# GraphSAGE aggregation: each broadcast of source indices for 28 buckets is split into two transfers of 14 buckets

## The chip, the core and the metric

The kernel runs on one core of a Trainium2 chip. The metric is the device time of one execution in microseconds (us). The core has a matrix engine (PE; its weight loads are listed apart as PEld), a vector engine (DVE), a scalar engine (ACT), GpSimd (POOL) and a sync engine (SP) that in this kernel does little but start DMA transfers. Sixteen DMA engines move all data between the memory (HBM) and the core's on-chip buffers; they also bring the instructions that the engines execute.

## What is computed

```python
def reference(x, src, dst, deg_inv, w_self, w_neigh):
    N = x.shape[0]
    nsum = _segment_sum(x[src], dst, N)
    h_neigh = nsum * deg_inv[:, None]
    return x @ w_self + h_neigh @ w_neigh
```

There are 12,500 nodes with 64 features and 800,000 edges. For each node the features of its in-neighbours are summed (gather by `src`, add by `dst`), scaled, multiplied by a 64x64 matrix, and added to the node's own features times another 64x64 matrix.

## The kernel before

The kernel sorts the edges into buckets and then does the gather and the sum with matrix products.

**Sort.** Each edge becomes a 32-bit key that holds its bucket: a block of 160 destination nodes and a block of 128 source nodes. 128 rows of keys are sorted on DVE and ACT (`sort_runs`), cut up, gathered again by indirect DMAs on POOL (`gather_runs`, L391), merged (`merge_runs`, L413 and L453), and cut into windows, one per bucket (`find_and_gather`, L603). This is done in two parts; part 0 is ready at about 815 us of the profiled execution, and part 1 is merged while the node sums already run.

**Lists in memory.** `decode_buckets` writes for each bucket 128 source positions as bf16 numbers to the tensor `sl` in memory (L652), 256 bytes per bucket, and keeps the destination positions on chip in `dlT`.

**Sums over nodes.** `nodes` walks over the 7,644 buckets in tiles of 8. For each tile PE does 8 products (L850) of a one-hot matrix of source positions (`ohs`) with a block of features (`xh`), which gathers the rows of 128 edges per bucket into the PSUM tile `ct`; ACT (L860) or, from tile 503 on, in turn DVE (L858) copies `ct` to `xg`; and PE does 16 products (L905) with the one-hot matrix of destination positions (`ohd`), which add the rows into the sums `acc`. Edges that did not fit a bucket come in as rows `lx`, gathered by POOL (L869) and added by L885. The finished sums go through `finish` (L968 to L976), which also loads `fo` on SP (L952) and stores `out`.

**One-hots, the place of the change.** `one_hots` makes both one-hot matrices for 28 buckets at a time, 273 times. SP starts a transfer (L819) that reads the 28 x 256 = 7,168 bytes of `sl` once for each of the 128 partitions, so that each partition of `slb` holds all 3,584 source positions; that is 128 rows of 7,168 bytes, or 896 KB. DVE then compares `slb` with the partition's number (L821, `ohs`) and `iota` with `dlT` (L824, `ohd`). `slb` has three buffers, so SP may run two groups ahead, and the transfer for a buffer is started when L821 of three groups earlier has ended.

**What sets the order.** From the merge on, the order of instructions on each engine is the order in which the program emits them (`manual_schedule` in `after_sort`). `nodes` yields once per tile, and between two yields `sums_and_merge` puts a portion of the merge of part 1, of its windows, of the decoding, or of the left-over edges. Waits between engines are on semaphores; each transfer that SP starts counts on one of eight semaphores, taken in turn.

Of the kernel before, what the change touches and what calls it, by code (L numbers as in the profile page):

```python
# [258 lines left out]
class Kernel:  # L259
# [552 lines left out]
    def one_hots(self, pool):  # L812


        nc = self.nc
        for c in range(0, NBID, 28):
            b = pool.tile([128, 28 * 128], BF, name="slb", bufs=3)
            src = self.sl[c:c + 28]
            nc.sync.dma_start(b, bass.AP(tensor=src.tensor, offset=src.offset, ap=[[0, 128], [1, 28 * 128]]))  # L819
            s = pool.tile([128, 28, 128], FH, name="ohs", bufs=3)  # L820
            nc.vector.tensor_scalar(s.rearrange("p c s -> p (c s)"), b, self.pidx[:, :1], None, op0=OP.is_equal)  # L821
            d = pool.tile([128, 14, HN, 2], FH, name="ohd", bufs=5)
            ix = self.dlT[:, c:c + 28].rearrange("p (c t) -> p c t", t=2)[:, :, None, :].to_broadcast([128, 14, HN, 2])
            nc.vector.tensor_tensor(d, self.iota[:, None].to_broadcast([128, 14, HN, 2]), ix, op=OP.is_equal)  # L824
            yield [(s[:, j], d[:, j // 2, :, j % 2]) for j in range(28)]
# [377 lines left out]
```

## Time and profile before

| | us |
|---|---|
| median of 3 runs (1891.56 to 1901.67) | 1899.85 |
| the profiled execution | 1899.66 |
| its span in the trace | 1897.9 |
| PE busy (matrix products) | 972.7 |
| DVE busy | 1672.6 |
| ACT busy | 1176.5 |
| POOL busy | 809.3 |
| first and last start of L819 | 821.6 and 1870.4 |

The profile is of one execution, in microseconds from the start of its span. Busy time is the time in which an engine executes; the share of busy time is an average over stages that have different limits. The first 815 us are the sort, in which PE does little; the sums over nodes take the rest. In that rest the DMA engines are mostly busy: the transfers of `slb` are by far the largest.

```profile
DMA  4322000001100012257677877889768887888884
...
slb<-sl SPq DMA_DIRECT2D x273, 896.0 KB
```

The first row gives, for 40 equal slices of the span, the mean busy share of the 16 DMA engines in tenths; the second the number and size of the transfers of L819. A row of waits names the engine that was idle, the line it was about to run, and what it was released by; "issue" there means that the profile shows nothing that it waited for. DMA queues are named by number: q1 holds what SP starts, q0 what POOL starts, q10 what ACT starts, and q8 and q14 instructions for the engines (187 packets of 16 KB and 62 of 8 KB).

### The profile page before, as it was taken

What the parts mean: (1) busy time and instruction counts of PE and PEld (TensorE: products, weight loads), DVE (VectorE), ACT (ScalarE), POOL (GpSimd) and SP (SyncE); (2) the same over time, 40 slices, a digit from 0 to 9 for tenths busy, and PEclk for the clock granted to TensorE, in tenths of its full rate; (3) what the DMA queues carried; (4) which work ended last, traced back from release to release, by engine and by line L of the source; (5) the groups of instructions that cost most, each with busy time, mean ns of one, the idle gap of its engine ahead of it and who ended that gap; (6) DMA issues with size and microseconds to landing.
All of it is one profiled execution on the core that took longest, in us unless ns stands there. A gap on an engine that the chain in (4) does not pass through costs nothing.

```text
span 1897.9 us, 54529 instructions
## 1 busy us (share of the span) xinstructions
PE 972.7 (51%) x23659; PEld 841.7 (44%) x23659; DVE 1672.6 (88%) x1760; ACT 1176.5 (62%) x1853; POOL 809.3 (43%) x917
## 2 busy tenths in 40 slices
PE   0043000000000000039888888898879989998997
PEld 0033000000000000038777777787768877787886
DVE  7999999997749998779699999999799888788885
ACT  7463019205510022549888898898968878777886
POOL 1000000699889984898521331326554123322431
PEclk9995555555555555569999999999989999999999
DMA  4322000001100012257677877889768887888884
GB/s 152 70 68 68 0 32 0 26 20 52 22 20 10 10 40 66 58 190 279 207 240 245 244 256 257 245 267 322 234 206 283 285 255 263 242 266 265 273 259 139
DMA packets 104804, 305.24 MB, mean 161 GB/s; under 512 B 52945, under 2 KB 60491, under 8 KB 103915
## 3 DMA queue, kind: packets, MB, share of 16 engines
q1 hardware_dynamic: 86347, 277.44, 41.2%
q0 software_dynamic: 17632, 22.17, 8.6%
q8 instruction: 187, 3.06, 0.6%
q10 hardware_dynamic: 576, 2.07, 0.3%
q14 instruction: 62, 0.51, 0.1%
HBM read 282.20 MB, written 19.41 MB: 159 GB/s over the span
## 4 chain that ended last, share of the span: by engine, by line
DVE 43%; PE 23%; POOL 16%; issue 11%; DMA 3%; ACT 3%; DVEq 0%; SPq 0%; POOLq 0%; ACTq 0%
DVE u L453 15%; PE ct L850 13%; POOL u L391 12%; PE acc L905 9%; DVE a L227 7%; DVE b L227 7%; DVE ohd L824 6%; DVE ohs L821 4%; POOL pad L304 2%; POOL v L603 1%; ACT xg L860 1%; DMA slb<-sl 1%; PE po L968 1%; DVE u L413 1%; POOL lx L869 1%
## 5 line engine op out<-in xcount | busy, mean ns | idle before, releaser
L860 ACT ACTIVATE xg<-ct 128x1024 f16<-128x1024 f32 (+1 forms) x898 | 853.3, 1032 | 166.8 <-PE ct L850 135.3
L850 PE MATMUL ct<-xh,ohs 128*128 128x128 f16 x7644 | 543.1, 223 | 64.3 <-DVE ohs L821 27.3
L850 PEld LDWEIGHTS <-ohs 128*128 128x128 f16 x7644 | 449.0, 100 | 107.7 <-issue 57.5
L391 POOL DMA_INDIRECT u<-d,ix x256 | 362.2, 1415 | 217.1 <-DVE ix L383 175.4
L905 PE MATMUL acc<-ohd,xg 64*128 64x80 f16 x15288 | 405.5, 199 | 72.8 <-issue 49.1
L453 DVE TENSOR_TENSOR u<-u 128x1456 f32<-128x1456 f32 (+46 forms) x292 | 393.7, 1377 | 21.6 <-issue 14.6
L905 PEld LDWEIGHTS <-xg 64*128 64x128 f16 x15288 | 318.6, 96 | 144.6 <-issue 70.4
L824 DVE TENSOR_TENSOR ohd<-iota,dlT 128x2240 f16<-128x2240 bf16 x273 | 360.2, 1319 | 0.0
L869 POOL DMA_INDIRECT lx<-xt,lsrc x140 | 236.8, 1691 | 263.2 <-PE acc L885 224.4
L821 DVE TENSOR_SCALAR ohs<-slb,pidx 128x3584 f16<-128x3584 bf16 x273 | 315.0, 1154 | 34.4 <-PE ct L850 21.7
L381 PE MATMUL stp<-idf,st 128*128 128x128 f32 x2 | 0.9, 447 | 356.8 <-DVE st L379 356.8
L227 DVE TENSOR_TENSOR a<-b 128x608 f32<-128x608 f32 (+44 forms) x124 | 174.0, 1445 | 4.6
L227 DVE TENSOR_TENSOR b<-a 128x608 f32<-128x608 f32 (+44 forms) x124 | 173.9, 1444 | 4.3
L976 POOL DMA_DIRECT2D out<-o x25 | 23.6, 946 | 354.7 <-DVE o L975 288.4
L381 PEld LDWEIGHTS stp<-idf,st 128*128 128x128 f32 x2 | 0.4, 182 | 357.3 <-issue 357.3
L660 PE MATMUL tr<-idb,l 128*128 128x128 bf16 x60 | 8.2, 278 | 285.2 <-issue 240.9
L858 DVE CAST xg<-ct 128x1024 f16<-128x1024 f32 x64 | 78.3, 1224 | 70.2 <-PE ct L850 69.5
L660 PEld LDWEIGHTS <-l 128*128 128x128 bf16 x60 | 5.0, 119 | 288.2 <-issue 244.3
L418 ACT ACTIVATE u<-u 128x30 f32<-128x30 f32 (+34 forms) x136 | 29.8, 268 | 143.6 <-DVE u L453 74.5
L229 ACT ACTIVATE b<-a 128x1 f32<-128x1 f32 (+21 forms) x52 | 18.7, 383 | 135.3 <-DVE a L227 130.2
L597 ACT ACTIVATE junk<-u,c 128x166 bf16<-128x166 f32 (+36 forms) x37 | 26.7, 722 | 119.1 <-DVE u L453 119.0
L603 POOL DMA_INDIRECT v<-d,ix x60 | 77.8, 1297 | 47.5 <-ACT ix L622 35.0
(153 smaller groups left out, 868.7 us busy)
## 6 DMA issues: line engine op xcount, KB each, us to landing
slb<-sl SPq DMA_DIRECT2D x273, 896.0 KB
u<-d,ix POOLq DMA_INDIRECT x256
xt<-xh SPq DMA_DIRECT2D x1, 3136.0 KB
fo<-own SPq DMA_DIRECT2D x26, 120.0 KB
own<-os SPq DMA_DIRECT2D x12, 256.0 KB
out<-o POOLq DMA_DIRECT2D x24, 120.0 KB
lx<-xt,lsrc POOLq DMA_INDIRECT x140
rd<-dst SPq DMA_DIRECT2D x4, 521.0 KB
```

The source lines that it names most:

```text
L227: nc.vector.tensor_tensor(view(dst, lo + sh, [[st, g], [1, l]]), x, y, op=op)
L304: self.nc.gpsimd.memset(self.pad, 0.0)
L391: nc.gpsimd.indirect_dma_start(out=u[:nr, EDGE + p * w:EDGE + (p + 1) * w], out_offset=None, in_=src, in_offset=bass.IndirectOffsetOnAxis( ...
L453: nc.vector.tensor_tensor(view(dst, EDGE + o + out, d), view(src, EDGE + o + x, d), view(src, EDGE + o + x + gap, d), op=op)
L603: self.nc.gpsimd.indirect_dma_start(out=self.v[:, k].bitcast(F32), out_offset=None, in_=flat(self.d2[home(part, k)], 128 * PITCH2[home(par ...
L821: nc.vector.tensor_scalar(s.rearrange("p c s -> p (c s)"), b, self.pidx[:, :1], None, op0=OP.is_equal)
L824: nc.vector.tensor_tensor(d, self.iota[:, None].to_broadcast([128, 14, HN, 2]), ix, op=OP.is_equal)
L850: nc.tensor.matmul(ct[:, i * 128:(i + 1) * 128], cols[i][0], self.xh[:, (b0 + i) % NB].rearrange("p a f -> p (a f)"), start=True, stop=True)
L858: nc.vector.tensor_copy(xg[:, :cnt * 128], ct[:, :cnt * 128])
L860: nc.scalar.activation(xg[:, :cnt * 128], ct[:, :cnt * 128], AF.Copy)
L869: nc.gpsimd.indirect_dma_start(out=x, out_offset=None, in_=self.xt, in_offset=bass.IndirectOffsetOnAxis(ap=self.left[p][1][:, c:c + 1], ax ...
L905: nc.tensor.matmul(acc[h][:, db % OCT * HN:(db % OCT + 1) * HN], xg[r, i * 128:(i + 1) * 128], d[r], start=db % OCT == 0 and sb == 0, stop ...
```

## The change

Each group's transfer is issued as two: the first brings the positions of the first 14 buckets into the first half of each partition of the `slb` buffer, the second those of the other 14 into the second half. Rows are 3,584 bytes long in place of 7,168, and there are 546 transfers of 128 rows in place of 273. Buffers, their number, and what is computed are unchanged.

```diff
         for c in range(0, NBID, 28):
             b = pool.tile([128, 28 * 128], BF, name="slb", bufs=3)
-            src = self.sl[c:c + 28]
-            nc.sync.dma_start(b, bass.AP(tensor=src.tensor, offset=src.offset, ap=[[0, 128], [1, 28 * 128]]))
+            for j in range(0, 28, 14):
+                src = self.sl[c + j:c + j + 14]
+                nc.sync.dma_start(b[:, j * 128:(j + 14) * 128],
+                                  bass.AP(tensor=src.tensor, offset=src.offset, ap=[[0, 128], [1, 14 * 128]]))
             s = pool.tile([128, 28, 128], FH, name="ohs", bufs=3)
```

All later lines of the kernel stand two lines lower than before. The order of instructions on PE, DVE, ACT and POOL is the same. On SP, at the start of the sums, the order before was (`fo` are the loads of `finish`):

```order
L652 DMA sl<-l_2277 128x128
L819 DMA slb<-sl 128x3584 x25
L952 DMA fo<-own 120x4x64
L819 DMA slb<-sl 128x3584 x4
L952 DMA fo<-own 120x4x64
L819 DMA slb<-sl 128x3584 x17
```

and it is now:

```order
L652 DMA sl<-l_2277 128x128
L820 DMA slb<-sl 128x1792 x50
L954 DMA fo<-own 120x4x64
L820 DMA slb<-sl 128x1792 x8
L954 DMA fo<-own 120x4x64
L820 DMA slb<-sl 128x1792 x34
```

Each transfer of a group has become two in the same place, and nothing has moved past them. On DVE, in the later part of the sums, two groups stood like this, with the semaphores that each instruction waits for in brackets (DMAHW are those of SP's transfers):

```order
L821 TENSOR_SCALAR ohs<-slb,pidx 128x3584 [waits DMAHW4_49]
L824 TENSOR_TENSOR ohd<-iota,dlT 128x2240
L877 TENSOR_SCALAR ohl<-wide,lp_2754 128x320
L821 TENSOR_SCALAR ohs<-slb,pidx 128x3584 [waits DMAHW5_49,PE_49]
L824 TENSOR_TENSOR ohd<-iota,dlT 128x2240
```

and stand now:

```order
L823 TENSOR_SCALAR ohs<-slb,pidx 128x3584 [waits DMAHW4_49,DMAHW3_49]
L826 TENSOR_TENSOR ohd<-iota,dlT 128x2240
L879 TENSOR_SCALAR ohl<-wide,lp_2760 128x320
L823 TENSOR_SCALAR ohs<-slb,pidx 128x3584 [waits DMAHW6_49,DMAHW5_49,PE_49]
L826 TENSOR_TENSOR ohd<-iota,dlT 128x2240
```

The comparison that makes `ohs` waits for one more semaphore, since it needs both halves.

## The prediction

> **What bounds the kernel now.** The change touches only the sums over nodes, from about 820 us on, so I read that part by stretches: busy time of each engine, then the waits, then the chain of work that ended last.
>
> ```profile
> core 0: us, PE busy (x) PEld busy (x) DVE busy (x) ACT busy (x) POOL busy (x), PEclk, DMA share, GB/s
> 1400.00:1500.00 100.00, 91.79 (x2285) 79.70 (x2285) 88.39 (x117) 79.44 (x91) 31.25 (x18) 0.95 0.75 257
> 1500.00:1600.00 100.00, 89.37 (x2340) 78.15 (x2340) 82.84 (x90) 80.08 (x89) 25.06 (x19) 1.00 0.81 265
> 1600.00:1700.00 100.00, 90.44 (x2254) 79.09 (x2252) 82.26 (x90) 76.43 (x84) 31.43 (x22) 0.95 0.83 257
> 1700.00:1800.00 100.00, 89.57 (x2359) 78.39 (x2357) 84.86 (x94) 80.95 (x88) 30.19 (x20) 1.00 0.85 270
> 1800.00:1890.00 90.00, 79.92 (x2070) 69.67 (x2068) 66.87 (x72) 72.38 (x80) 22.30 (x15) 0.98 0.69 212
> 1000.00:1270.00 270.00, 233.57 (x5976) 204.02 (x5974) 269.69 (x246) 234.85 (x268) 68.32 (x34) 0.97 0.80 252
> ```
>
> From 1000 to 1270 us, where the merge of part 1 runs beside the sums, DVE is busy for 269.69 of 270 us: nothing that frees another engine helps there. From 1400 us on no engine is full, PE is nearest (441 of 490 us, the sum of its five rows), and the DMA engines are busy for 0.69 to 0.85 of the time. What PE waits for in that stretch is this (line, releaser: us in total, times, longest):
>
> ```profile
> PE acc L905 <- issue: 25.0, 30, 2.4
> PE ct L850 <- issue: 14.8, 9, 3.2
> PE ct L850 <- ACT xg L860: 1.7, 7, 0.3
> ```
>
> 441 busy and 39.8 us of "issue" make 481 of 490: PE is the bound, and its only large wait is one for which the profile names no releaser. The chain of waits of the same stretch runs over PE too, and its longest pieces are such waits:
>
> ```profile
> 1553.86 2.49 issue
> 1734.33 3.17 issue
> ```
>
> What PE lacks there is its instructions. The page counts them and the packets that bring them:
>
> ```profile
> PE 972.7 (51%) x23659; PEld 841.7 (44%) x23659; DVE 1672.6 (88%) x1760; ACT 1176.5 (62%) x1853; POOL 809.3 (43%) x917
> ...
> q8 instruction: 187, 3.06, 0.6%
> ```
>
> 2 x 23,659 instructions over 187 packets is 253 for each packet of 16 KB; that q8 serves PE I take from PE having nine tenths of all instructions. PE runs some 22,600 instructions (both x columns) from 1400 to 1890 us, 89 packets' worth, and stops 39 times, for 1.02 us on average. So nearly every second packet comes late.
>
> Why late? Here is a stretch of 10 us: two gathers that POOL issues and two of PE's stops, then the packets of each DMA queue in four windows, 1554.3 to 1557, 1557 to 1558, 1559.1 to 1560.8 and 1560.8 to 1562 us (packets, MB, share of the time of 16 engines).
>
> ```profile
> 1552.94 1.33 POOL L869 DMA_INDIRECT lx<-xt,lsrc  x1 [4.22 <-PE acc L885]
> 1559.63 0.95 POOL L869 DMA_INDIRECT lx<-xt,lsrc  x1 [5.36 <-PE acc L885]
> ...
> 1556.34 0.23 PE L850 MATMUL ct<-xh,ohs 128*128 128x128 f16 x1 [2.49 <-issue]
> ...
> 1563.11 0.29 PE L905 MATMUL acc<-ohd,xg 64*128 64x80 f16 x6 [1.85 <-issue]
> ```
>
> ```profile
> q1 hardware_dynamic: 124, 0.86, 94.4%
> ...
> q1 hardware_dynamic: 36, 0.15, 68.9%
> q0 software_dynamic: 31, 0.03, 59.1%
> ...
> q1 hardware_dynamic: 90, 0.54, 75.5%
> ...
> q0 software_dynamic: 22, 0.03, 36.1%
> q1 hardware_dynamic: 5, 0.03, 5.7%
> q8 instruction: 1, 0.02, 4.9%
> ```
>
> The gather issued at 1552.94 us (done on POOL at 1554.27) has no packet at all while the rows of an `slb` transfer move; its packets come when the transfer ends, after 1557. The next one, and the one instruction packet, again come only after 1560.8, when q1 runs dry, and PE's stop at 1563.11 follows. The DMA engines do not alternate row by row: **other queues get their turn when a transfer's rows on an engine, 8 of 128, are through.** A row takes 0.944 x 16 x 2.7 / 124 = 0.33 us, so a turn of `slb` lasts about 2.6 us. Each instruction packet that is asked for during a turn waits for its end.
>
> [...]
>
> **The change part by part.**
>
> *Turns of half the length (gain).* 8 rows of 3,584 bytes take half of 2.6 us, so an instruction packet waits up to 1.3 us less. The 30 stops at L905 average 0.83 us and would mostly go; the 9 at L850 average 1.64 us and would shrink to about a fifth. If every late packet met a whole turn, 30 x 0.75 + 9 x 1.3 = 34 us would go; many meet part of one, or two. I take two thirds of 39.8 us, **-27 us**, between 0 (turns do not shorten) and -39.8. Room for it is there: in 463 us DVE's 405 us (sum of its five rows) are 88% and ACT's 389 us 84%. From 1000 to 1270 us the same cure is worth 0, since DVE is full.
>
> ```profile
> PE acc L905 <- issue: 7.9, 11, 2.2
> ...
> 844.00 2.44 DMA u<-d,ix
> ...
> 1351.88 6.29 DMA tk<-d
> ```
>
> Between 1270 and 1400 us PE has 7.9 us of the same waits (first row), and the chain has a small load of POOL that takes 6.29 us (third row, 7 KB): POOL's queue waits for turns as well. PE is only partly the bound there; I take **-3 us**, between 0 and -11. The gathers before the merge end with 2.44 us of DMA on the chain (second row): **-1 us**, between 0 and -2.4.
>
> *273 more transfers to issue (cost).* Rows for this and the next points: the issue itself, what SP waits for, what DVE waits for at L821, semaphore instructions there, the start of the sums, and a window (115 to 140 us) with rows of 256 bytes only.
>
> ```profile
> L819 SPq DMA_DIRECT2D slb<-sl x273: 319/320/516, 821.6 to 1870.4; - x137
> SPq L819 <- DVE ohs L821: 819.5, 254, 10.0
> DVE ohs L821 <- DMA slb<-sl: 9.9, 4, 5.0
> L821 DVEq EVENT_SEMAPHORE  x214: 21/21/50, 817.9 to 1875.7; - x107
> 826.42 1.15 DVE L821 TENSOR_SCALAR ohs<-slb,pidx 128x3584 f16<-128x3584 bf16 x1 [5.01 <-DMA slb<-sl]
> 829.32 1.22 DVE L821 TENSOR_SCALAR ohs<-slb,pidx 128x3584 f16<-128x3584 bf16 x1 [0.51 <-DMA slb<-sl]
> ...
> q1 hardware_dynamic: 10651, 2.71, 42.2%
> ```
>
> 273 x 0.32 = 87 us on SP, which waits 819.5 us at this line: hidden. Behind it in SP's queue stand only the loads `fo` and the next groups. The second half is issued 0.32 us after the first, whose rows move for 1.3 us, so it is not late: 0. Without that cover each group would land 0.32 us later, 87 us over 273 groups.
>
> *Twice the rows (cost).* The 256-byte rows take 0.422 x 16 x 25 / 10,651 = 0.016 us each, which bounds the fixed part of a row from above; below, it is 0. 273 x 128 more rows are at most 0.13 us per group on each engine, 35 us in all beside a period of (1870.4 - 821.6) / 272 = 3.86 us per group. The DMA share would go from 0.8 to at most 0.84. What hides it is the lead of two groups: 269 of 273 groups were there when DVE wanted them. Exposed is the first group, for which DVE waits 5.01 us, and the next: **+0.5 us**; a late landing here and there, **+1 us**; if the cover were gone, +35.
>
> *One more semaphore at L821 (cost).* At most 273 x 0.05 = 14 us. DVE has 214 such instructions at L821 now and is yet busy 269.69 of 270 us, so they run under the instruction before: 0. Behind L821 stand L824 and the copies L858, for which PE waits; exposed, all 14 would count.
>
> **Sum**, against the profiled execution's own 1899.66 us, which is the median of the runs (1899.85) within 0.2: -27 - 3 - 1 + 0.5 + 1 = -29.5, **1870 us**.
>
> [...]
>
> **The rivals.**
>
> *No change: the turn is not a transfer.* If an engine counts rows or bytes and takes both halves in one turn when both are queued (the second is queued after 0.32 us, so they always are), instruction packets wait as long as before and only +0.5 + 1 is left: **1901 us**. For it: the rows above show transfers of 8 rows per engine and cannot tell a limit of 8 rows from one of 16. Against: in the four windows the other queues come in when a transfer is through, though the next groups follow closely.
>
> *Slower: the second half is held up by the turns it gives away.* Every group now yields once in its middle. A turn of POOL's queue is priced by this stretch (1500 to 1700 us):
>
> ```profile
> q0 software_dynamic: 1347, 1.82, 11.4%
> ```
>
> 0.114 x 16 x 200 / 1,347 = 0.27 us; with 0.13 for the rows, 0.4 us per group. It decides where DVE reaches L821 with less than that in hand. If a third of the groups did, 91 x 0.4 = 36 us is lost at L821, DVE falls behind PE, and half of the gain (13) is left: **1923 us**. Against: only 4 waits for `slb` in the row above, and 2 of them are at the start.
>
> *Much slower: the fixed part of a transfer is paid twice in a row.* The first group takes 826.42 - 821.6 = 4.8 us, the next lands 2.9 us after it; 1.9 us are fixed. Were halves to run one after the other, a group would take 2 x 1.9 + 2.9 = 6.7 us where DVE takes one every 3.86: 273 x 2.9 = 780 us more, **2680 us**. Against: the second group already overlaps the first's fixed part. [...]
>
> **How the numbers follow.** Forecast 0.67, no change 0.19, held up 0.13, paid twice 0.01. The forecast's own range is 1852 (all of 39.8, 6 more before 1400) to 1889. A measurement of this kernel can tell about 0.5%, 9.5 us, from no change. Faster by more is the forecast but for its weak end: 0.66; within: 0.21; slower: 0.13. The range that holds 8 in 10 goes from 1852 over the no-change case: 1852 to 1904.
>
> **What would show it.** Right: PE's "issue" waits from 1400 us on fall from 39.8 to some 13 us, their longest from 3.2 to under 2; PE's busy share there rises over 0.94; gathers' packets appear between the halves; 1000 to 1270 us keeps its length. Wrong: the same "issue" waits (rival one), or `slb` as releaser of L823 tens of times (rival two). The prediction falls if instruction packets are late for another reason than turns, or if DVE or ACT, at 88% and 84%, take over before PE has gained.

## The result and the profile after

The change makes the kernel slower by about 0.8%: a median of 1916.28 us over 10 runs (1906.84 to 1931.02) against 1901.03 us over 10 runs of the kernel before (1891.56 to 1906.39), a ratio of 1.0079 with a 95% interval from 1.0054 to 1.0103. The prediction said 1870 us and a range of 1852 to 1904. The profiled execution of the change took 1915.36 us, 15.7 more than that of before; its span is 1913.6 us.

The busy time of each engine by stretches, as shown for the kernel before:

```profile
core 0: us, PE busy (x) PEld busy (x) DVE busy (x) ACT busy (x) POOL busy (x), PEclk, DMA share, GB/s
1400.00:1500.00 100.00, 83.75 (x2143) 73.24 (x2139) 89.53 (x143) 75.52 (x85) 35.67 (x21) 0.95 0.79 251
1500.00:1600.00 100.00, 87.78 (x2222) 77.33 (x2223) 78.86 (x85) 76.28 (x85) 25.29 (x18) 0.96 0.82 254
1600.00:1700.00 100.00, 87.29 (x2258) 76.47 (x2257) 80.43 (x89) 76.95 (x86) 32.12 (x19) 0.98 0.81 248
1700.00:1800.00 100.00, 87.35 (x2237) 76.70 (x2235) 81.95 (x90) 76.99 (x83) 29.12 (x21) 0.95 0.84 262
1800.00:1890.00 90.00, 82.90 (x2149) 72.95 (x2147) 75.56 (x83) 73.72 (x80) 27.09 (x19) 0.98 0.85 262
1000.00:1270.00 270.00, 231.92 (x5996) 201.70 (x5988) 269.73 (x245) 239.11 (x272) 62.06 (x34) 0.98 0.81 251
```

DVE is as full from 1000 to 1270 us as it was (269.73 of 270). From 1400 us on PE is busy for 429 of 490 us, where it was 441: its share fell from 0.90 to 0.88 and did not rise over 0.94. (These stretches are the same in time, not in work: the change reaches each group of buckets some microseconds later.)

The waits of that same stretch in the change (line, releaser: us in total, times, longest):

```profile
ACT xg L862 <- PE ct L852: 100.4, 121, 4.1
DVE xg L860 <- PE ct L852: 76.0, 45, 4.7
...
PE acc L907 <- issue: 30.8, 22, 3.1
...
PE ct L852 <- issue: 15.9, 13, 2.9
```

PE's waits without a releaser are 46.7 us in place of 39.8. This view lists 35 of them in place of 39, but it counts short waits of other kinds too. The stops can also be counted where a block of 256 PE instructions ends (weight loads and products together). The traces show this length: there is one packet on q8 for every 253 PE instructions (47,318 over 187), and from 1400 to 1890 us 26 of the 43 gaps over 0.4 us in PE's weight loads stand at one and the same place in a count of 128 weight loads in the kernel before, 35 of 43 in the change, and no other place has more than two. In time, 39.0 of the 49.2 us of such gaps in the later part of the sums stand at the ends of blocks in the kernel before, 52.6 of 64.9 in the change. With gaps of 0.15 us or more, the change has 42 such stops in place of 30 in this stretch (worked out from the two traces). The two longest pieces without a releaser on the chain of waits are about as long as before (3.17 and 2.60 there):

```profile
1581.61 3.13 issue
...
1747.79 2.86 issue
```

To see where the 15.7 us lie, the starts of the `ohs` comparison (L821, now L823) can be compared group by group, since the program does the same in both. Worked out from the two traces, in us:

```
groups         before   change
0 to 36         150.8    155.4
36 to 108       278.0    278.0
108 to 144      149.1    151.6
144 to 272      474.9    482.5
```

The stretch in which DVE is full keeps its length to a tenth. In the first row gathers of `lx` land late: on the chain from 822 to 965 us three of them take 5.5 to 6.4 us in the change, and one of 6.1 in the kernel before. A second execution of the change has only one (6.4 us), and its first row is 151.4 us. The loss that stays is in the last two rows (152.2 and 480.2 us in that second execution), above all in the last, in which PE is the bound.

### The profile page after: what moved, and what is told of

Read it like the earlier page. It is cut to its first block, busy times and chain, and to the rows that moved or that the text cites. A ratio compares the mean times of both kernels' runs of the same rounds, so it can differ in the third digit from the quotient of the medians.

```text
span 1913.6 us, 54933 instructions
## 1 busy us (share of the span) xinstructions
PE 961.0 (50%) x23659; PEld 835.5 (44%) x23659; DVE 1672.0 (87%) x1760; ACT 1178.6 (62%) x1853; POOL 808.0 (42%) x917
## 4 chain that ended last, share of the span: by engine, by line
DVE 41%; PE 24%; POOL 15%; issue 11%; DMA 5%; ACT 3%; DVEq 0%; SPq 0%; ACTq 0%; POOLq 0%
DVE u L453 14%; PE ct L852 13%; POOL u L391 12%; PE acc L907 9%; DVE a L227 7%; DVE b L227 7%; DVE ohd L826 6%; DVE ohs L823 4%; POOL pad L304 2%; DMA slb<-sl 2%; ACT xg L862 1%; DVE u L413 1%; DMA lx<-xt,lsrc 1%; DMA rd<-dst 1%; PE acc L887 1%
## 5 line engine op out<-in xcount | busy, mean ns | idle before, releaser
L907 PE MATMUL acc<-ohd,xg 64*128 64x80 f16 x15288 | 400.5, 200 | 70.0 <-issue 46.5
L907 PEld LDWEIGHTS <-xg 64*128 64x128 f16 x15288 | 317.3, 96 | 137.7 <-issue 59.6
L823 DVE TENSOR_SCALAR ohs<-slb,pidx 128x3584 f16<-128x3584 bf16 x273 | 314.1, 1151 | 40.9 <-PE ct L852 32.1
```

The source lines that it names most:

```text
L907: nc.tensor.matmul(acc[h][:, db % OCT * HN:(db % OCT + 1) * HN], xg[r, i * 128:(i + 1) * 128], d[r], start=db % OCT == 0 and sb == 0, stop ...
```

## The experiments

Each kernel ran beside the kernel before on the same chip, in five rounds or three, and each diff is against the kernel before unless it says otherwise.

### What a repetition gives

The kernel before, unchanged (same_again), and the change once more (halves_again):

> The kernel before, unchanged, for a second profile and as the zero of the scale. Every theory: ratio 1.000 within 0.003. It shows how much PE's waits for issue from the 144th group on differ between two profiles of one program (39.8 us in the first).

> The change as it stands, for a second profile. Ratio 1.008. If the loss is late instructions (theory Q: with two transfers per group some DMA engine has rows of queue 1 at nearly any time, so what the instruction queue brings comes later), PE's waits for issue at the ends of 256-instruction blocks from group 144 on are over 50 us again, against 40 to 42 in the two profiles of the kernel before. If they are near 41, Q does not carry the loss.

same_again: 1899.14 us, ratio 0.9990 (0.9961 to 1.0019). halves_again: 1916.81 us, 1.0088 (1.0053 to 1.0123). The loss is real. The stops at the ends of blocks in groups 144 to 272 come to 48.9 us in halves_again, just under the 50 that was asked for (53.8 in the first execution of the change, 40.1 and 41.7 in the two of before). One trace alone is a weak witness, though. The waits of PE in same_again and then in halves_again, from 1400 us on:

```profile
PE acc L905 <- issue: 26.0, 19, 2.8
...
PE ct L850 <- issue: 9.4, 8, 2.2
```

```profile
PE acc L907 <- issue: 32.4, 29, 2.2
...
PE ct L852 <- issue: 8.9, 10, 1.9
```

Two executions of before give 39.8 and 35.4 us, two of the change 46.7 and 41.3: the direction holds, and a difference of 5 us between two single traces says nothing.

### Are the stops caused by the `slb` transfers at all?

no_slb transfers the positions of the first three groups only and leaves out the other 270 transfers.

```diff
-            b = pool.tile([128, 28 * 128], BF, name="slb", bufs=3)
...
-            nc.sync.dma_start(b, ...)
+            if c < 84:
+                b = pool.tile([128, 28 * 128], BF, name=f"slb{c}")
...
+                nc.sync.dma_start(b, ...)
+                held = [b] if c == 0 else held + [b]
+            b = held[c // 28 % 3]
```

> Only the first three groups' positions are transferred; the other 270 groups compare the same three buffers again, so that the transfers are left out and the values are not those of the reference. If the transfers of queue 1 are what makes instructions late: PE's waits for issue from group 144 on fall from 40 us to under 10, and the time falls by 35 to 60 us (ratio 0.97 to 0.98). If instructions are late for another reason: the waits stay near 40 us and the ratio is 0.995 to 1.000, since DVE waits for the transfers in 4 to 6 groups only.

1838.02 us, 0.9666 (0.9619 to 0.9712). PE's products have no wait without a releaser left from 1400 us on. Two of its stretches:

```profile
1500.00:1600.00 100.00, 99.29 (x2676) 88.46 (x2670) 96.72 (x107) 90.25 (x100) 44.82 (x26) 1.00 0.16 20
1600.00:1700.00 100.00, 98.92 (x2671) 88.09 (x2668) 95.58 (x104) 91.60 (x102) 36.49 (x22) 1.00 0.14 15
```

PE is busy for 99% and the DMA engines for 15% (next to last column). So this part of the prediction holds: the stops come from the traffic of `slb`, and all of it is worth 3.3%, or 64 us, a little more than the 35 to 60 that were expected.

### Row length, second issue, number of parts

One transfer with rows of half the length (rows_half; `slb` has a gap of 128 bytes between the halves, so that the rows stay apart):

```diff
-            nc.sync.dma_start(b, bass.AP(..., ap=[[0, 128], [1, 28 * 128]]))
+            nc.sync.dma_start(b[:, :, :14 * 128], bass.AP(..., ap=[[0, 128], [14 * 128, 2], [1, 14 * 128]]))
```

> One transfer per group as before, but each partition's 7,168 bytes go into two pieces 128 bytes apart, so that a transfer has 256 rows of 3,584 bytes as the two halves have together; one issue, one semaphore per group. Theory R (the shorter rows cost DMA time, and what other queues bring comes later): ratio 1.008 like the change, queue 1 busy near 43.8%. Theory T (the number of transfers: issues, completions, semaphores, one more wait on DVE): ratio 1.000.

1901.04 us, 1.0001 (0.9978 to 1.0025): twice the rows of half the length cost nothing.

Two transfers of 27 buckets and of 1 (uneven; `for lo, hi in ((0, 27), (27, 28))` in place of the halves):

> Two transfers per group, 27 buckets and 1 bucket: issues, completions, semaphores and waits are as many as in the change, but the first is nearly the whole and the second is short. Theory S (the second semaphore, the second issue): ratio 1.006 to 1.008. Theory Q (rows of two transfers keep the DMA engines out of step): about a third of it, 1.000 to 1.004.

1901.77 us, 0.9997 (0.9973 to 1.0021): a second issue, a second completion and a second semaphore cost nothing.

Four transfers of 7 buckets (four_parts):

> Four transfers of 7 buckets per group: rows of 1,792 bytes, 1,092 transfers. Both R and T: the loss of the change, 0.8%, comes about three times, ratio 1.02 to 1.027; queue 1 busy near 49%. If the loss is not in the number of rows or transfers but was chance, or has to do with halves alone: ratio 1.00 to 1.01.

1907.72 us, 1.0051 (1.0021 to 1.0081): a loss, but not a larger one than with two.

The whole transfer and a second small one, of 256 bytes per partition that nobody reads (extra):

> The group's transfer in one piece, and a second transfer of the last bucket again to a buffer that nobody reads: the issue and the completion of a second transfer without a second semaphore at L821; it reads 9 MB more. Theory S by the semaphore on DVE: ratio 1.000. By the issue or completion itself: 1.006 to 1.008. Theory Q: 1.000 to 1.004, like the uneven halves.

1941.83 us, 1.0176 (1.0119 to 1.0233). This was expected by neither theory, and uneven has a small transfer of the same shape and loses nothing. The loss comes as late instructions again (48 stops at the ends of blocks, 65.7 us, in the table further down); what makes them late here was not found.

### Partitions in place of columns

The group split into partitions 0 to 63 and 64 to 127, whole rows (parts_half, the first diff), and into even and odd partitions (parity, the added lines of the second):

```diff
-            nc.sync.dma_start(b, bass.AP(..., ap=[[0, 128], [1, 28 * 128]]))
+            for h in range(0, 128, 64):
+                nc.sync.dma_start(b[h:h + 64], bass.AP(..., ap=[[0, 64], [1, 28 * 128]]))
```

```diff
+            for h in range(2):
+                nc.sync.dma_start(b[h::2], bass.AP(..., ap=[[0, 64], [1, 28 * 128]]))
```

> Two transfers per group, but split by partitions: 64 rows of 7,168 bytes each, so rows are as many and as long as before; two issues, two completions, two semaphores. Theory T: ratio 1.008 like the change. Theory R: ratio 1.000, queue 1 busy near 41.2%.

> Two transfers of 64 rows of 7,168 bytes: the first for the even partitions, the second for the odd ones. Each reads all 7 KB and is spread over all partitions, where parts_half (1.1325) gave each transfer 64 neighbouring partitions. Theory of the address: rows take as long as before (mean 312 ns, median 272) and the time is 0.997 to 1.004. Rival (two equal transfers cost): 1.005 or more. If half the number of rows per transfer is what made parts_half slow, rows take some 500 ns here too and the time is 1.10 or more.

parts_half: 2148.02 us, 1.1325 (1.1290 to 1.1361), which neither theory had. A row takes 528 ns (median of all) where it took 272. PE's waits in it, from 1400 us on:

```profile
PE acc L907 <- issue: 75.0, 34, 4.9
...
PE ct L852 <- issue: 21.2, 12, 4.7
...
DVE ohs L823 <- DMA slb<-sl: 5.5, 5, 1.9
```

Even here, DVE hardly waits for `slb` (5.5 us in this stretch). The loss comes in the main as late instructions: 96 us of PE's waits in this stretch, against 40. Earlier, from 980 to 1300 us, where DVE was full before, it now waits for PE's `ct` for 39.6 us. Why a row to one of 64 neighbouring partitions took 528 ns is not shown.

parity: 1899.32 us, 0.9991 (0.9959 to 1.0023). Its rows have the median of before, 272 ns. So two equal transfers of 448 KB, as large as those of the change, lost nothing here, where each row is whole (0.9991 against 1.0079).

### Does the distance between the halves matter?

My first theory for the loss was the queue: an instruction packet waits for all that queue 1 has queued on its engine, and two halves queued together fill more of it. In spaced, the halves are two buffers, DVE compares one, makes `ohd`, and compares the other; close is the same with the two comparisons together.

> The halves are two buffers here. DVE compares the first half, then makes ohd, then compares the second half; each half's transfer is started when its own comparison of three groups earlier has ended, so the two transfers of a group start some 1.9 us apart in place of 0.36. Bytes, rows and transfers are those of the change; DVE has 273 more comparisons of half the length. Theory of the queue (an instruction packet waits for every row that is already queued on its engine's queue 1, and two transfers queued together keep more engines busy at a time): with the second half not yet queued, a packet asked for during the first half waits only for that; PE's issue waits from 1400 us on fall below the 39.8 us of before, to some 20 to 30 us, and the time is 0.985 to 1.000 of before, where the extra comparisons cost up to 0.003. Rival (a transfer of 3,584-byte rows holds the engines in a costlier way wherever it stands): the issue waits stay at 45 us or more and the time at 1.007 to 1.012.

> The same two buffers and the same 273 more comparisons as the kernel with spaced halves, but the two comparisons of a group follow each other and ohd comes after them, so the two transfers of a group start some 0.6 us apart and are queued together most of the time. It prices the added comparisons and the split buffers. Theory of the queue: it loses like the change, 1.006 to 1.014, with 45 us or more of issue waits from 1400 us on. Rival (the distance between the halves does not matter): it agrees with the spaced kernel within 0.3%.

spaced: 1932.69 us, 1.0154 (1.0120 to 1.0188). close: 1941.43 us, 1.0178 (1.0142 to 1.0215). Both miss, because I had mis-priced the added comparisons. The groups of `ohs` in spaced:

```profile
L822 DVE TENSOR_SCALAR ohs<-slb,pidx 128x1792 f16<-128x1792 bf16 x273 | 187.7, 688 | 32.7 <-PE ct L854 18.2
L827 DVE TENSOR_SCALAR ohs<-slb,pidx 128x1792 f16<-128x1792 bf16 x273 | 186.2, 682 | 0.4 <-DMA slb<-sl 0.4
```

187.7 + 186.2 = 373.9 us of DVE, against 315.0 for the whole comparisons: 59 us more, in a kernel in which DVE is the bound for 270 us. PE's waits from 1400 us on are 40.4 us in spaced and 54.9 in close, but the first is in neither of the ranges that were set for it, and the times agree within 0.3%. The two kernels cannot tell the theories apart. So I delayed the transfers with waits alone, and left DVE as it was (the diff is against the change; in apart, only the second half waits; in later, `if len(ohds) >= 3`, both):

```diff
+        ohds = []
...
-                nc.sync.dma_start(b[:, j * 128:(j + 14) * 128], ...
+                dma = nc.sync.dma_start(b[:, j * 128:(j + 14) * 128], ...
+                if j and len(ohds) >= 3:
+                    self.tc.add_manual_dep(dma.ins, ohds[-3].ins.name, ...)
...
-            nc.vector.tensor_tensor(d, ...)
+            ohds.append(nc.vector.tensor_tensor(d, ...))
```

> The change, with nothing added on DVE, PE, ACT or POOL: the transfer of the first half starts as in the change, when L823 of three groups earlier has ended; that of the second half also waits for the ohd comparison L826 behind it, so it starts about 1.9 us after the first in place of 0.36. Theory of the queue (a packet waits for every row that queue 1 has queued on its engine when it is asked for; two halves queued together also keep more engines at work at a time): the loss of the change goes, 0.990 to 1.002 of before, and PE's issue waits from 1400 us on are 25 to 40 us, against 46.7 in the change. Rival (a transfer split in equal halves costs this wherever its second half stands): 1.005 to 1.012 and 45 us or more.

> The control: both halves wait for L826 as well, so they start as late as the second half does in the kernel before this, but 0.36 us apart as in the change. If starting later is what helps or harms, this agrees with the kernel before it within 0.3%. Theory of the queue: it is like the change, 1.005 to 1.012 with 45 us or more of issue waits from 1400 us on, and at least 0.5% above the kernel before it.

apart: 1924.71 us, 1.0081 (1.0057 to 1.0105). later: 1916.87 us, 1.0052 (1.0028 to 1.0076). In apart the second half is issued 1.23 us after the first (median of groups 144 to 272), not the 1.9 that were meant, but well over the 0.36 of the change and of later. The loss is all there, and the theory falls. PE's waits in apart, from 1400 us on, are 52.1 us, not the 25 to 40 that it asked for:

```profile
PE acc L911 <- issue: 40.6, 47, 2.7
...
PE ct L856 <- issue: 11.5, 11, 3.0
```

### What the rows read

All rows of a transfer read the same bytes of the list: 7 KB before, 3.5 KB in the change. rows_half has the short rows and reads 7 KB with one transfer. The next three kernels change only what is read. same_half, against rows_half:

```diff
-            nc.sync.dma_start(b[:, :, :14 * 128], bass.AP(..., ap=[[0, 128], [14 * 128, 2], [1, 14 * 128]]))
+            nc.sync.dma_start(b[:, :, :14 * 128], bass.AP(..., ap=[[0, 128], [0, 2], [1, 14 * 128]]))
```

distinct and then cross, both against the change:

```diff
-                src = self.sl[c + j:c + j + 14]
+                src = self.sl[c % 1120 + 128 * j:c % 1120 + 128 * (j + 14)]
...
-                                  bass.AP(..., ap=[[0, 128], [1, 14 * 128]]))
+                                  bass.AP(..., ap=[[14 * 128, 128], [1, 14 * 128]]))
```

```diff
-                src = self.sl[c + j:c + j + 14]
+                src = self.sl[c:c + 28]
...
-                                  bass.AP(..., ap=[[0, 128], [1, 14 * 128]]))
+                                  bass.AP(..., ap=[[0, 64], [14 * 128, 2], [1, 14 * 128]]))
```

> One transfer per group of 256 rows of 3,584 bytes, as in rows_half, but both rows of a partition read the first 14 buckets: the one-hots of the other 14 are made from the wrong positions, and every row of a transfer reads the same 3,584 bytes. Theory of the address (rows go slower when all engines read the same 3.5 KB at a time than when they read over 7 KB): rows average 165 ns or more as in the change (168.6; rows_half 159), and the time is 1.004 to 1.011 of before. Rival (it is the second transfer of equal size that costs, whatever it reads): like rows_half, 159 ns and 0.997 to 1.003.

> Two transfers of 128 rows of 3,584 bytes, as in the change, but each partition reads another 3,584 bytes of the first 4,736 buckets, so no two rows of a group read the same bytes; the one-hots are made from wrong positions. Theory of the address: rows average 160 ns or less and the time is at most 1.002 of before, and lower if even 7 KB read by all engines is slow. Rival: rows of 165 ns or more and 1.005 to 1.011.

> Two transfers of 128 rows of 3,584 bytes as in the change, but in each the even partitions read the first 14 buckets and the odd ones the other 14, so that the rows of one transfer read over 7 KB; the one-hots of odd partitions in the first half and of even ones in the second are made from the wrong positions. Theory of the address, in the form that same_half leaves (what all engines read at a time spans 3.5 KB): rows average 162 ns or less and the time is 0.997 to 1.003 of before. Rival (two transfers of 128 rows of half the length cost this whatever they read, as distinct suggests): 165 to 173 ns and 1.004 to 1.010.

same_half: 1969.08 us, 1.0353 (1.0312 to 1.0395). The theory had the direction, but its range ended at 1.011. It differs from rows_half (1.0001) in the source address of half the rows and in nothing else of the traffic. PE's waits in it, from 1400 us on, are 62 us, where rows_half has 33:

```profile
PE acc L907 <- issue: 47.9, 29, 5.2
...
PE ct L852 <- issue: 14.2, 11, 3.6
```

```profile
PE acc L907 <- issue: 21.3, 15, 2.4
...
PE ct L852 <- issue: 12.0, 10, 2.4
```

cross: 1904.10 us, 1.0011 (0.9983 to 1.0039). It has the transfers, the rows and the semaphores of the change, but each transfer reads over 7 KB, and the loss is gone; its interval and those of the change do not meet. One thing more differs: an issue takes SP 0.56 us in place of 0.34 (medians of groups 144 to 272), which sets the halves further apart. apart, with 1.23 us between them, speaks against that as the reason.

distinct: 1911.07 us, 1.0053 (1.0024 to 1.0081). Here no two rows share a byte, and the theory asked for 1.002 at most. It missed.

The time that a row takes, from the packets of groups 144 to 271 in each trace (ns):

```
                 mean   median   9 of 10 under
before          312.8     272      361
parity          327.5     272      440
rows_half       159.6     140      154
cross           165.4     140      174
distinct        166.7     140      167
change          166.7     140      229
same_half       193.1     173      267
```

Reading the same 3.5 KB twice in one transfer lengthened the typical row (173 against 140 ns). In the change only the slower rows are longer, and the mean, on which I had set the bounds for cross (162 ns or less), does not tell it from cross.

### Is there something left to gain?

If 7 KB is narrow too, a wider source should make the kernel before faster. two_sources lets odd partitions read elsewhere in the list; two_copies writes the list twice and computes everything as before:

```diff
-        self.sl = self.dram.tile([NCOL, 128], BF, name="sl")
+        self.sl = self.dram.tile([2, NCOL, 128], BF, name="sl")
...
-            rows = self.sl[BASE[part]:BASE[part] + 128 * kpr].rearrange(...)
+            rows = self.sl[:, BASE[part]:BASE[part] + 128 * kpr].rearrange(...)
-            (nc.gpsimd if part else nc.sync).dma_start(rows[:, k:k + n], l16[:, :n])
+            (nc.gpsimd if part else nc.sync).dma_start(rows[:, :, k:k + n], l16[:, None, :n].to_broadcast(...))
...
-            src = self.sl[c:c + 28]
-            nc.sync.dma_start(b, bass.AP(..., ap=[[0, 128], [1, 28 * 128]]))
+            src = self.sl[0, c:c + 28]
+            nc.sync.dma_start(b, bass.AP(..., ap=[[0, 64], [NCOL * 128, 2], [1, 28 * 128]]))
```

> One whole transfer per group as before, but the odd partitions read their 7,168 bytes from a place 2,240 buckets further on, so that the rows of a transfer read over 14 KB in two places; the one-hots are made from wrong positions. It asks whether the address theory, which explains the change (3.5 KB: 1.0079 and 1.0088; 7 KB in two transfers: 1.0011), has something left to give before the change too. If 7 KB is still narrow: rows average under 300 ns (312 before) and the time is 0.988 to 0.997. If 7 KB is wide enough: 0.997 to 1.003 and 305 to 320 ns.

> The list sl is written twice, by the same 16 transfers with twice the bytes; even partitions read the first copy, odd ones the second, in one whole transfer per group. Everything is computed as before. If two_sources' 0.9955 comes from the wider reading: 0.990 to 0.998 of before, and PE's issue waits from 1400 us on 30 to 39 us (37.4 in two_sources, 39.8 before). If it comes from reading a list that was written long before, or is chance: 0.998 to 1.003.

two_sources: 1902.44 us, 0.9955 (0.9924 to 0.9986), with rows of 322.9 ns, not shorter ones; the time is in the range that was set for a gain, the rows are not. two_copies: 1903.83 us, 0.9971 (0.9941 to 1.0001), with 41.2 us of PE's waits, not fewer. The times lean to a gain of 0.3%, which is not established; no kernel here beats the one before clearly.

## Why the prediction was wrong

*The bound and its cause: held.* PE's stops are late instructions and they come from the transfers of `slb`: without them there are none (no_slb: 0 stops in the table below, where before has 30). The time follows them. For groups 144 to 272, the stops of PE at every 256th instruction (gaps of 0.15 us or more in its weight loads) against the length of the stretch, from one trace of each kernel in which DVE does the same work; the last column is explained under the next step:

```
               stops   us of stops   us of the   mean us to
                                      stretch    the packet
no_slb             0        0.0        420.1        0.44
rows_half         28       38.5        466.0        2.36
uneven            36       44.8        471.1        2.47
cross             36       44.1        471.6        2.61
before again      33       41.7        473.1        2.36
two_sources       34       38.0        473.1        2.39
before            30       40.1        474.9        2.36
parity            39       47.7        475.2        2.55
two_copies        35       40.9        477.3        2.46
four_parts        52       56.2        478.8        2.82
later             35       40.9        479.7        2.50
change again      47       48.9        480.2        2.73
distinct          50       55.0        481.4        2.69
change            41       53.8        482.5        2.73
apart             47       54.5        497.2        2.79
extra             48       65.7        505.3        2.94
same_half         52       84.0        524.9        3.37
parts_half        64      137.6        606.9        4.00
```

Counted from no_slb, a microsecond of stops costs between 1.0 and 1.5 us, over a range of 187 us, in kernels that differ in the transfers of the lists alone. For differences as small as that of the change, 5 to 8 us in this stretch, single rows do not decide: parity has more stops than before and the same length, and later has the stops of before and a longer stretch (in it DVE waits 6.7 us for `slb` from 1400 us on). The prediction took 39 of 89 packets to be late, "nearly every second"; counted at the ends of blocks from 1400 to 1890 us it is 30 of 89, every third.

*"Turns of half the length (gain)": the step that failed.* It gave -27 us, 0 to -39.8. The waits grew by 7 us in the profiled execution, and by 6 between the second executions of both kernels. The step took from the windows around 1557 us that other queues come in when one transfer is through, and that a shorter transfer lets an instruction packet in sooner. Its 8 rows on an engine were my estimate, 128 rows spread evenly over 16 engines: no view here names the engine of a packet. Here is the place of the change's longest stop. Two halves are issued from 1579.57 us on (first fence, SP's instructions); then the packets of each queue from 1580 to 1582.2 and from 1582.2 to 1583.4 us; then PE:

```profile
1579.57 0.80 SPq L820 DMA_DIRECT2D slb<-sl  x2
```

```profile
q1 hardware_dynamic: 240, 0.75, 90.0%
q0 software_dynamic: 38, 0.04, 10.9%
...
q1 hardware_dynamic: 54, 0.17, 40.7%
q0 software_dynamic: 13, 0.01, 9.5%
q8 instruction: 1, 0.02, 5.3%
```

```profile
1584.74 0.24 PE L907 MATMUL acc<-ohd,xg 64*128 64x80 f16 x3 [3.13 <-issue]
```

In this place POOL's queue gets its turns while queue 1 is at 90%, as the prediction said it would (38 packets of q0; there were none from 1554.3 to 1557 before). Over the 77 gathers of `lx` in groups 144 to 271 little of that is left: the next packet of POOL's queue comes 0.97 and 0.96 us after the gather on average in two executions of before, 0.89 and 0.96 in two of the change. Only the longest of these waits shortened (nine in ten were under 2.76 and 2.62 us and are under 1.93 and 2.01).

The instruction packet does not come sooner. PE enters its last block before the stop at 1577.15 us, and the next packet starts at 1582.31, 5.16 us later, after both halves have been issued and queue 1 has come down from 90%. The traces hold the instruction packets (187 on q8 in each), so this wait can be measured for all 85 to 87 blocks of groups 144 to 272 (one block is 256 PE instructions): from PE's first weight load in one block to the start of the packet that ended last before its first weight load in the next. Without the `slb` traffic it is 0.44 us on average. That these packets are PE's, and that the stops hang on them, shows in the 151 late blocks of two executions of before and two of the change: the packet ended 1.05 to 1.63 us before PE went on, every time. The mean wait is 2.36 us in both executions of before and 2.73 in both of the change (last column above). Single waits spread by 1.2 to 1.4 us (standard deviation), so each of these means is good to about 0.15 us. The step said up to 1.3 us less; the runs exclude that and show some 0.4 us more. With the halves set apart it is 2.79 us (apart). So in these runs instruction packets did not get in when one shorter transfer was through; the rule was read from POOL's packets and a single instruction packet in a stretch of 10 us. By what rule an instruction packet does get in is not shown.

*What was left out: a cost of the split itself.* The sum had none besides the issue, the rows and the semaphore. Those three were right at next to nothing where they stand alone (uneven 0.9997, rows_half 1.0001). In the change the bound on the rows broke: two rows of 166.7 ns take 20.6 ns more than one of 312.8, where the bound was 16; in rows_half it is 6.4. The loss was gone where each transfer reads 7 KB, by whole rows (parity 0.9991), by rows from both halves (cross 1.0011), or by one transfer (rows_half 1.0001), and it was there where each reads 3.5 KB or less (the change 1.0079, halves_again 1.0088, apart 1.0081, later 1.0052, four_parts 1.0051), four times as large where the same 3.5 KB are read twice in one transfer (same_half 1.0353). That the loss hangs on what the rows of a transfer read is therefore shown by two pairs, same_half with rows_half and the change with cross. That a narrow range is the reason is not shown, nor is how it acts. In same_half the rows are longer (193.1 ns on average, rows_half 159.6); in the change, hardly (166.7, cross 165.4). distinct reads 448 KB per transfer and loses 0.5% all the same, extra has a whole transfer over 7 KB in each group and loses 1.8%, and four_parts should lose more than the change and does not (1.0051 against 1.0079). Either the address effect has a second side, which these kernels do not separate, or distinct and extra lose for reasons of their own.

*Smaller terms.* The waits from 1270 to 1400 us, for which the prediction had -3 us, did not fall:

```profile
PE acc L907 <- issue: 8.3, 7, 2.3
...
PE ct L852 <- issue: 2.3, 2, 1.7
```

That is 8.3 at L907 where it was 7.9 at L905. The gathers before the merge, with -1 us, end with 3.14 us of DMA on the chain (4.97 in the second execution), where it was 2.44:

```profile
844.33 3.14 DMA u<-d,ix
```

The exposed costs held: DVE waits for `slb` 8.7 us in 3 times (9.9 in 4 before; the longest of them 5.3 us where the first was 5.01, so +0.3 for the predicted +0.5), and the row of SP shows that its cover is still there.

```profile
DVE ohs L823 <- DMA slb<-sl: 8.7, 3, 5.3
```

```profile
SPq L820 <- DVE ohs L823: 746.9, 269, 10.6
```

At three places the cover was thinner than that: the chain from 1400 to 1890 us of the profiled execution has three transfers of `slb`, 17.4 us in all, so DVE came to L823 with no time in hand there. The second execution of the change has none on its chain and loses the same, and cross has two and loses nothing, so this is not the loss.

```profile
1457.16 4.24 DMA slb<-sl
...
1667.51 7.14 DMA slb<-sl
...
1676.66 6.06 DMA slb<-sl
```

*The rivals.* "No change: the turn is not a transfer" pointed at the step that failed and gave 1901 us; what it lacked is the cost of the split. Its own mechanism, both halves in one turn because both are queued, is not shown either: apart issues the second half 1.23 us later and the instruction packets come no sooner (2.79 us against 2.73 in the change and 2.36 before). "Held up" named the sign, but not by its mechanism: L823 waited 3 times for `slb`, not 91. The profile could not have told the gain from its absence, as the prediction itself said of the rows of before; the chance of 0.67 was too high for a step that rested on one stretch of 10 us, read in the main from another queue than the one it was about.

## What to carry to other kernels

When an engine stops for its instructions, take the traffic away once before designing a cure: no_slb prices the whole effect (3.3%) and shows the cause, and only then is it worth asking which property of the traffic matters. Do not carry a rule on how one DMA queue gets its turn to another: measure the packets of the queue in question. Their mean wait (2.36 and 2.73 us) kept the two kernels apart in both executions here, where the sum of PE's waits differed by 5 us between two executions of one kernel. No split of this broadcast gained anything here. Where one has to be split, the runs speak for transfers that each read the whole source into every second partition (even and odd partitions: 0.9991), and against columns (1.0079) and neighbouring partitions (1.1325).

## What the runs showed of the hardware that was not expected

- 256 rows that all read the same 3,584 bytes made the kernel 3.5% slower than 256 rows of the same length that read two such ranges in turn (same_half 1.0353, rows_half 1.0001).
- Transfers to 64 neighbouring partitions took 528 ns for a row of 7,168 bytes where those to even and odd partitions took 272, and the price appeared in the main as late instructions on PE, not as late data (parts_half 1.1325, parity 0.9991; mean wait for an instruction packet 4.00 and 2.55 us).
- Where PE stopped at the end of a block of 256 instructions, an instruction packet had ended 1.05 to 1.63 us before it went on (all 151 late blocks of before, same_again, the change and halves_again). On average such a packet started 0.44 us after PE had entered the block before without the broadcasts, and 2.36 us after with them (no_slb, before).
- A small transfer of 256 bytes per partition, read by nobody, cost 1.8% beside a whole one (extra, 1.0176), while the same small transfer as a part of the group cost nothing (uneven, 0.9997). This stays open.
